# Gated linear attention followed by a dropless mixture of experts: row stores half a pair later, the early gather sooner, first expert units between the last rows

## The chip, the cores and the metric

The kernel runs on one core of a Trainium2 chip. The core has a matrix engine (TensorE, PE in the profile), a vector engine (VectorE, DVE), an activation engine (ScalarE, ACT), a general engine (GpSimd, POOL) and a queue engine that starts most transfers (SyncE, SP). Each engine runs its own instructions in program order and waits where an operand or a buffer is not ready. The metric is the device time of one execution in microseconds, and a smaller number is better. Three executions of the kernel before gave 453.42, 454.57 and 455.56 us.

## The reference

There are two stages. The first is a recurrence with a decaying state for each of 4 x 8 heads, 768 steps and a head size of 48. The second sends each of the 3072 result rows, 384 wide, to one of eight experts.

```python
# first stage, per batch b and head h
for t in range(S):
    state = alpha[t][:, None] * state + outer(k[t], v[t])
    y[t] = q[t] @ state
# x: [4 * 768, 8 * 48], the heads of a token side by side
logits = x @ w_gate                       # [3072, 8]
e = argmax(logits); gate = softmax(logits)[e]
out = gate * (relu(x @ w1[e]) @ w2[e])    # w1[e]: 384 x 1024, w2[e]: 1024 x 384
```

Every token is computed by its expert, however many tokens one expert gets.

## The kernel before

**The attention stage.** The 3072 tokens are cut into NT = 24 chunks of 128, six to a batch element. For each chunk the kernel loads four tiles of 128 x 8 x 48 float32: `a` (alpha), `k`, `q` and `v`. The load of a head row of a token is a piece of 192 bytes. `logs` takes the logarithm of alpha on ScalarE, `cums` sums it over the chunk with a matmul into the one PSUM bank `cum` and makes two exponentials of it (`icp`, `cp`), `operands` multiplies k and q with these on GpSimd, `transposes` turns both with TensorE into the PSUM tile `tp`, from where ScalarE copies kT and VectorE copies qT. `scores` makes kT x qT in the banks `sA` and `sB`; VectorE masks the first into dA, ScalarE copies the second to dB and GpSimd masks it. `products` makes k x v of the chunk, again in `sA` or `sB`, and `state` (GpSimd) folds it into the state `U`. The last row of `cp` goes through DRAM and comes back in another layout: `decay_out` and `decay_in`, both started by ScalarE, so ScalarE waits in `decay_in` until `decay_out` has landed.

**Pairs.** Chunks are worked on two at a time. The loop `for s in range(2, NT - 2, 2)` at L688 emits, for the pair s and s + 1: `reads` (q x state, L408), `weighs` (v x masked scores, L420), `products` of s + 1 and s + 2 (L442), the scores of later chunks, and `rows` (L468), which brings the results back to token order in the one PSUM bank `xr`. `keep_rows` copies a chunk's 128 x 392 rows, with the eight negated logits behind them, to the tile `xs` (ScalarE L475, GpSimd L476); `store_rows` (L481) writes them to the DRAM tensor `x_rows`, and waits for both copies. Everything is emitted by hand in the order in which it is to run on each engine (`manual_schedule`).

**Loads and stores share one queue.** All loads of a, k, q, v, the stores of rows and the weights of the experts are started by SyncE, in the order of the program. `some_loads` names the first ones; after that, `more_loads(n)` takes the next n from the list `to_load`, once at the start of a pair (L689) and once in its middle (L731). Buffers are five deep for a, k and q and six for v.

**Routing.** Chunks form groups of four, with the last four in two groups of two. `choose` finds the expert of each token and `ohs`, the running count per expert (GpSimd, L494). `rank_products` makes the rank of each token within its expert by two matmuls (L499, L500), `slots_of` the slot (VectorE), `one_hots` two 0/1 matrices per chunk, and `tokens_of_slots` multiplies these (L569) so that `slots` (L585) can read off which token stands in which slot. The first two blocks of the first expert are filled from the first sixteen chunks alone: `early_slots` finds them (L531, L537) in pair s = 20, and `fetch_lot(0)` gathers their rows from `x_rows` with two indirect transfers that GpSimd starts (L267).

**The last pair and the experts.** After the loop comes the pair s = 22 (L758 to L826). Between its steps stand the ranks of the last groups, the turning of the two early blocks (L780), and `first_layer` (L796), a generator that emits the first expert layer on the two early blocks, 24 matmuls of 256 columns in eight groups; `go_ahead(n)` takes n steps of it. `fetch_lot(1)` then gathers the other six blocks of that lot, and expert by expert follow `layer1` (L939), `layer2` (L955), `turn_block` (L931) and the scattered stores of the results (L961).

`keep_busy(n)` (L593) is n matmuls of zeros into the `xr` bank, whose results nobody reads.

Of the kernel before, what the change touches and what calls it, by code (L numbers as in the profile page):

```python
# [8 lines left out]
F32 = mybir.dt.float32  # L9
# [9 lines left out]
def kernel(  # L19
# [265 lines left out]
    with tc.tile_pool(name="ld", bufs=6) as ld, \  # L285
# [20 lines left out]
        def some_loads(names):  # L306
            for n in names.split():
                load(n[0], int(n[1:]))


        to_load = [(n, x) for s in range(7, NT + 2) for n, x in (("k", s), ("q", s), ("a", s + 1), ("v", s - 2))]

        def more_loads(n):
            for _ in range(min(n, len(to_load))):
# [2 lines left out]
        def logs(s):  # L317
            st[s]["ln"] = work.tile([C, H, D], F32, name="ln")
            nc.scalar.activation(st[s]["ln"][:], st[s]["a"][:], AF.Ln)
# [38 lines left out]
        def transposes(s):  # L358
            d = st[s]
            for i, n in enumerate(("kT", "qT")):  # L360
                tp = ps.tile([C, NP, C], F32, name="tp", bufs=2)
                for p in range(NP):
                    nc.tensor.transpose(tp[:, p, :], pair(kqb[s % 4][:, i], p), ident[:])  # L363
                d[n] = work.tile([C, NP, C], F32, name=n, bufs=2 + i)
                if i:
                    nc.vector.tensor_copy(d[n][:], tp[:])  # L366
                else:
                    nc.scalar.copy(d[n][:], tp[:])

        def scores(s):  # L370
            d = st[s]
            sA = ps.tile([C, NP, C], F32, name="sA")
            sB = ps.tile([C, NP, C], F32, name="sB")
            for p in range(NP):
                for t, r in ((sA, 0), (sB, DP)):
                    nc.tensor.matmul(  # L376
                        t[:, p, :], lhsT=d["kT"][r : r + D, p, :], rhs=d["qT"][r : r + D, p, :], start=True, stop=True,
                    )
            d["dA"] = work.tile([C, NP, C], F32, name="dA")
            nc.vector.tensor_tensor(d["dA"][:], sA[:], cmask[:, None, :].to_broadcast([C, NP, C]), op=ALU.mult)  # L380
            d["dB"] = work.tile([C, NP, C], F32, name="dB")
            nc.scalar.copy(d["dB"][:], sB[:])
            nc.gpsimd.affine_select(
                d["dB"][:], d["dB"][:], compare_op=ALU.is_ge, fill=0.0,
                base=0, pattern=[[0, NP], [1, C]], channel_multiplier=-1,
            )
# [47 lines left out]
        def products(s):  # L434

            d = st[s]
            if s >= NT or s % NB + 1 == NB:
                return
            kv = ps.tile([C, NP, C], F32, name="s" + "BA"[s % 2])[:, :, :D]
            for p in range(NP):  # L440
                for i, r in enumerate((0, DP)):
                    nc.tensor.matmul(  # L442
                        kv[r : r + DP, p, :], lhsT=kqb[s % 4][:, 0, 2 * p + i, :], rhs=d["v"][:, 2 * p + i, :D],
                        start=True, stop=True,
                    )
            d["acc"] = work.tile([C, NP, D], F32, name="acc" + "BA"[s % 2], bufs=1)
            if s % 2:
                nc.vector.tensor_tensor(d["acc"][:], kv, st[s - 1]["U"][:, :, :D], op=ALU.add)  # L448
            else:
                nc.scalar.copy(d["acc"][:], kv)  # L450
# [20 lines left out]

        def keep_rows(s):
            d = st[s]
            xs = work.tile([C, W], F32, name="xs")
            nc.scalar.copy(xs[:, :Dm].rearrange("t (p c) -> t p c", p=NP), d["xr"][:, :, :D2])  # L475
            nc.gpsimd.tensor_copy(xs[:, Dm:], lgn[:, s, :])  # L476
            d["xs"] = xs
# [146 lines left out]
        operands(1)  # L624
        decay_in(0)
        scores(0)
        some_loads("v1 k2 q2 a3 v2")
        logs(2)
        products(0)
        transposes(1)  # L630
        cums(2)
        decay_out(1)
        operands(2, q=None)
# [1 line left out]
        scores(1)  # L635
        operands(2, None, nc.vector)
        logs(3)
        decay_in(1)
        some_loads("a4 k3 q3 a5 k4")
        decay_out(2)  # L640
        y = results_of(0)
# [10 lines left out]
        transposes(2)  # L652
        cums(3)
        rows(0)
        decay_in(2)
        keep_rows(0)
        operands(3)
        scores(2)
        logs(5)
        state(1)  # L660
        cums(4)
        rows(1)
        decay_out(3)
        some_loads("q4 a6 v3 k5 q5")
        store_rows(0)
        keep_rows(1)
        operands(4)
        transposes(3)
        logs(6)
# [2 lines left out]
        decay_in(3)  # L672
        transposes(4)
        decay_out(4)
        some_loads("v4 k6 q6 a7")
        store_rows(1)
        operands(5)
        cums(6)
        decay_in(4)
# [6 lines left out]
        late_consts(1)  # L686
        parts = fetch_parts(0)
        for s in range(2, NT - 2, 2):  # L688
            more_loads(4 + (s % 6 == 2))  # L689
            y = results_of(s)  # L690
            reads(s)
            reads(s + 1)

            weighs(s, 0)
            weighs(s, 1)
            products(s + 1)
            products(s + 2)
            weighs(s + 1, 0)
            results_to(s, y, 0)
            weighs(s + 1, 1)  # L700
            results_to(s, y, 1)
            state(s + 1)
            state(s + 2)
            do(logs, s + 5)
            scores(s + 2)
            do(logs, s + 6)
            do(cums, s + 5)
            ranks = y[0][:].rearrange("r i p t -> r (i p t)")
            for g in groups_of:
                if g[-1] == s - 1:  # L710
                    slots_of(*rank_products(g, ranks[:, : len(g) * E]))
            counts = ranks[:, C : C + E]
            if s in (TE, ORD):

                nc.tensor.matmul(
                    counts, lhsT=ones_sq[:], rhs=ohs[:, s, :], start=True, stop=True, skip_group_check=True,
                )
            if s == TE + 4:
                early_slots(ranks[:, 2 * C : 2 * C + EB * NQ])
            transposes(s + 3)  # L720
            do(operands, s + 5)
            rows(s)
            keep_rows(s)
            store_rows(s)
            for _ in range(min(2 * (s == ORD), len(hots))):
                one_hots(hots.pop(0))
            do(cums, s + 6)
            do(transposes, s + 4)
            do(decay_out, s + 5)
            do(decay_in, s + 4)  # L730
            more_loads(4 + (s % 6 == 0))  # L731
            rows(s + 1)
            keep_rows(s + 1)
            store_rows(s + 1)
            do(operands, s + 6)
            if s == TE:
                close_early(counts[0:1, 0:1])
            if s == ORD:
                turns(counts[0:1, :])
            scores(s + 3)  # L740
            do(decay_out, s + 6)
            do(decay_in, s + 5)
            late_consts(s)
            late_consts(s + 1)
            for _ in range(min(1 + (s < ORD), len(hots))):
                one_hots(hots.pop(0))
            if s == TE + 4:
                fetch_lot(0)
            for g in groups_of:
                if g[-1] == s + 1:  # L750
                    choose(g)

            for _ in range(6 if s > NT - 6 else 4 if s > NT - 10 else 0):
                next(parts, None)
        for _ in parts:
            pass

        s = NT - 2  # L758
        xT[0] = early.tile([C, DB, CAP], F32, name="xT")
# [2 lines left out]
        y = results_of(s)  # L762
        reads(s)
        reads(s + 1)
        n = len(groups_of[-2]) * E
        r = rank_products(
            groups_of[-2], ps.tile([C, NP, D2 + E], F32, name="xr")[:].rearrange("r p t -> r (p t)")[:, :n],
        )
        weighs(s, 0)
        weighs(s, 1)  # L770
        weighs(s + 1, 0)
        results_to(s, y, 0)
        weighs(s + 1, 1)
        results_to(s, y, 1)
        slots_of(*r)
        one_hots(hots.pop(0))
        for k in range(EB):
            tp = ps.tile([C, NP, C], F32, name="tp", bufs=2)
# [5 lines left out]
        keep_rows(s)  # L784
        store_rows(s)
        tokens_of_slots(NT - 8, NT - 4)
        rows(s + 1)
        keep_rows(s + 1)
        store_rows(s + 1)
        choose(groups_of[-1])  # L790
        while hots:
            one_hots(hots.pop(0))
        banks.close()
        mps = ctx.enter_context(tc.tile_pool(name="moe_ps", bufs=2, space=PSUM))

        def first_layer():  # L796
            for f in range(FB):
                hp = mps.tile([C, CAP], F32, name="hp", bufs=3)
                for a in range(DB):
                    nc.tensor.matmul(  # L800
                        hp[:, :EC], lhsT=w_t[0][0][:, a, f * C : (f + 1) * C], rhs=xT[0][:, a, :EC],
                        start=(a == 0), stop=(a == DB - 1),
                    )
                    yield
                nc.scalar.activation(h_t[0][:, f, :EC], hp[:, :EC], AF.Relu)

        ahead = first_layer()

        def go_ahead(n):
            for _ in range(n):  # L810
                next(ahead, None)

        go_ahead(1)
        slots_of(*rank_products(groups_of[-1], mps.tile([C, Dm], F32, name="zp")[:, : 2 * E]))
        tokens_of_slots(NT - 4, NT - 2)
        go_ahead(6)
# [284 lines left out]
```

## Time and profile before

| what | before |
|---|---|
| median of three executions | 454.57 us |
| span of the profiled execution | 456.1 us |
| TensorE matmuls busy | 428.9 us (94%) |
| GpSimd busy | 142.8 us (31%) |
| VectorE busy | 138.3 us (30%) |
| ScalarE busy | 108.9 us (24%) |
| transfers | 59.41 MB, mean 130 GB/s |

The share of TensorE is that of the whole span. Cut into stages it reads differently: from 183.3 us to the end, the experts, 266.95 of 272.70 us are busy, and from 0 to 183.3 us, the attention stage and the crossing to the experts, 161.98 of 183.30 us. The clock that the throttle granted to TensorE is a column of its own: it is full but for a few stretches of 3.4 or 6.8 us. A wait is printed with the engine that waits and the last thing that it waited for; SPq is the queue of SyncE.

### The profile page before, as it was taken

What the parts mean: (1) busy time and instruction counts of PE and PEld (TensorE: products, weight loads), DVE (VectorE), ACT (ScalarE), POOL (GpSimd) and SP (SyncE); (2) the same over time, 40 slices, a digit from 0 to 9 for tenths busy, and PEclk for the clock granted to TensorE, in tenths of its full rate; (3) what the DMA queues carried; (4) which work ended last, traced back from release to release, by engine and by line L of the source; (5) the groups of instructions that cost most, each with busy time, mean ns of one, the idle gap of its engine ahead of it and who ended that gap; (6) DMA issues with size and microseconds to landing.
All of it is one profiled execution on the core that took longest, in us unless ns stands there. A gap on an engine that the chain in (4) does not pass through costs nothing.

```text
span 456.1 us, 7755 instructions
## 1 busy us (share of the span) xinstructions
PE 428.9 (94%) x2981; PEld 289.6 (63%) x2981; DVE 138.3 (30%) x411; ACT 108.9 (24%) x230; POOL 142.8 (31%) x256
## 2 busy tenths in 40 slices
PE   7989688999999579999999999999999999999994
PEld 5768577888888568855555455665555555555452
DVE  5334344567676643363101110211111101111100
ACT  4455342454553212111011011110110111111011
POOL 2277666557665405015015011005111010010011
PEclk9899998899999979999999999999999999999998
DMA  9994687698985352199554260082270040000000
GB/s 163 180 198 90 141 175 164 127 195 168 206 191 134 99 192 74 36 368 399 184 205 118 86 227 29 1 293 75 67 289 34 1 154 34 1 31 17 2 31 30
DMA packets 128434, 59.41 MB, mean 130 GB/s; under 512 B 110462, under 2 KB 123320, under 8 KB 128394
## 3 DMA queue, kind: packets, MB, share of 16 engines
q1 hardware_dynamic: 116258, 48.87, 41.3%
q0 software_dynamic: 3328, 9.94, 6.6%
q10 hardware_dynamic: 8808, 0.08, 1.1%
q8 instruction: 24, 0.39, 0.4%
q14 instruction: 16, 0.13, 0.1%
HBM read 49.30 MB, written 9.96 MB: 130 GB/s over the span
## 4 chain that ended last, share of the span: by engine, by line
PE 51%; issue 29%; POOL 7%; DMA 7%; DVE 2%; SPq 2%; ACT 1%; POOLq 0%; ACTq 0%
PE zp L955 15%; PE hp L939 13%; PE xr L468 4%; PE sA L376 4%; PE tp L363 4%; PE cum L330 3%; DMA vb<-in_v_dram 3%; PE hp L800 3%; POOL out_dram L961 3%; PE y L420 2%; DMA q_sb<-in_q_dram 1%; SPq L304 1%; DMA xg<-x_rows,g_idx 1%; POOL xg L267 1%; PE xtp L931 1%
## 5 line engine op out<-in xcount | busy, mean ns | idle before, releaser
L955 PE MATMUL zp<-w,h_sb 128*128 128x384 f32 (+2 forms) x560 | 137.1, 487 | 0.0
L939 PE MATMUL hp<-xT,w 128*128 128x416 f32 (+3 forms) x384 | 125.2, 486 | 0.5 <-DVE xT L933 0.5
L955 PEld LDWEIGHTS zp<-w,h_sb 128*128 128x128 f32 (+2 forms) x560 | 73.6, 163 | 56.4 <-issue 14.8
L939 PEld LDWEIGHTS hp<-xT,w 128*128 128x128 f32 x384 | 71.6, 190 | 52.8 <-issue 38.7
L961 POOL DMA_INDIRECT out_dram<-zo,o_idx x26 | 25.8, 994 | 220.7 <-ACT zo L960 195.2
L944 DVE TENSOR_SCALAR h_sb<-hp 128x416 f32<-128x416 f32 (+3 forms) x32 | 17.9, 558 | 149.0 <-PE hp L939 138.5
L960 ACT ACTIVATE zo<-zp,gw 128x384 f32<-128x384 f32 x26 | 15.1, 581 | 123.6 <-PE zp L955 119.1
L946 ACT ACTIVATE h_sb<-hp 128x416 f32<-128x416 f32 (+3 forms) x32 | 15.7, 491 | 106.7 <-PE hp L939 99.3
L376 PE MATMUL sA<-qT,kT 48*128 48x128 f32 x192 | 28.9, 291 | 0.7 <-DVE accA L448 0.5
L376 PE MATMUL sB<-qT,kT 48*128 48x128 f32 x192 | 28.6, 291 | 0.1
L267 POOL DMA_INDIRECT xg<-x_rows,g_idx x26 | 25.2, 971 | 9.8 <-issue 7.2
L420 PE MATMUL y<-dA,vb 128*64 128x128 f32 x192 | 28.1, 292 | 0.0
L354 POOL TENSOR_TENSOR kqb<-k_sb,icp 128x384 f32<-128x384 f32 x23 | 23.0, 1000 | 15.7 <-ACT icp L333 15.7
L376 PEld LDWEIGHTS sA<-qT,kT 48*128 48x128 f32 x192 | 24.0, 193 | 6.0 <-issue 2.7
L363 PE MATMUL tp<-ident,kqb 128*128 128x128 f32 x192 | 27.2, 287 | 0.6 <-POOL kqb L356 0.3
L420 PE MATMUL y<-dB,vb 128*64 128x128 f32 x192 | 27.3, 293 | 0.0
L933 DVE COPY xT<-xtp 128x384 f32<-128x384 f32 (+3 forms) x29 | 13.1, 485 | 46.1 <-PE xtp L931 45.8
L468 PE MATMUL xr<-back,yT 128*128 128x104 f32 x192 | 25.5, 276 | 1.6 <-ACT xs L475 1.6
L363 PEld LDWEIGHTS tp<-ident,kqb 128*128 128x128 f32 x192 | 23.1, 148 | 6.1 <-issue 2.7
L468 PEld LDWEIGHTS xr<-back,yT 128*128 128x128 f32 x192 | 23.7, 193 | 3.0 <-ACT xs L475 2.4
L366 DVE COPY qT<-tp 128x512 f32<-128x512 f32 x24 | 16.6, 691 | 25.8 <-PE tp L363 25.7
L376 PEld LDWEIGHTS sB<-qT,kT 48*128 48x128 f32 x192 | 23.9, 193 | 0.3 <-ACT accB L450 0.3
(172 smaller groups left out, 439.9 us busy)
## 6 DMA issues: line engine op xcount, KB each, us to landing
w<-in_moe_w_dram SPq DMA_DIRECT2D x14, 1536.0 KB
x_rows<-xs SPq DMA_DIRECT2D x24, 196.0 KB
a_sb<-in_alpha_dram SPq DMA_DIRECT2D x24, 192.0 KB
k_sb<-in_k_dram SPq DMA_DIRECT2D x24, 192.0 KB
q_sb<-in_q_dram SPq DMA_DIRECT2D x24, 192.0 KB
vb<-in_v_dram SPq DMA_DIRECT2D x24, 192.0 KB
w<-in_moe_w_dram SPq DMA_DIRECT2D x12, 128.0 KB
w<-in_moe_w_dram SPq DMA_DIRECT2D x8, 192.0 KB
```

Of the source, the lines that this page charges most:

```text
L267: nc.gpsimd.indirect_dma_start(out=xg[:, j, :], out_offset=None, in_=x_d[: N + 1 if n else TE * C + 1, :], in_offset=bass.IndirectOffsetOn ...
L354: k.tensor_tensor(kq[:, 0, :, :D], d["k"][:], heads(d["icp"]), op=ALU.mult)
L363: nc.tensor.transpose(tp[:, p, :], pair(kqb[s % 4][:, i], p), ident[:])
L366: nc.vector.tensor_copy(d[n][:], tp[:])
L376: nc.tensor.matmul(t[:, p, :], lhsT=d["kT"][r : r + D, p, :], rhs=d["qT"][r : r + D, p, :], start=True, stop=True,)
L420: nc.tensor.matmul(d["y"][h][at(p, a) : at(p, a) + DP, n, :], lhsT=d["v"][:, 2 * p + a, :], rhs=d["d" + "AB"[a]][:, p, :], start=(first an ...
L468: nc.tensor.matmul(xr[:, p, :], lhsT=d["yT"][:, p // (NP // 2), p % (NP // 2), :], rhs=back[:, p, :], start=True, stop=True)
L939: nc.tensor.matmul(hp[:, c0:c1], lhsT=w1[:, a, f * C : (f + 1) * C], rhs=xT[:, a, c0:c1], start=(a == 0), stop=(a == DB - 1),)
L944: nc.vector.tensor_relu(h[:, f, c0:c1], hp[:, c0:c1])
L946: nc.scalar.activation(h[:, f, c0:c1], hp[:, c0:c1], AF.Relu)
L955: nc.tensor.matmul(zp[i * wd : (i + 1) * wd, :], lhsT=h[:, f, c : c + wd], rhs=w2[:, f, :], start=(f == 0), stop=(f == FB - 1), skip_group ...
L961: ins = nc.gpsimd.indirect_dma_start(out=out[:, :], out_offset=bass.IndirectOffsetOnAxis(ap=idx, axis=0), in_=zo[:], in_offset=None, bound ...
```

## The change

The edits fall into four kinds. Stores of rows are moved down in the program: `store_rows(s)` and `store_rows(s + 1)` stand half a pair later, `xs` gets a third buffer for that, and the loads are listed with alpha first and taken as 4 + 5 in each pair. In the first pairs, `transposes(1)` goes ahead of `products(0)`, three `keep_busy` matmuls stand ahead of it, and two `decay_in` are moved down. In pair s = 20, `fetch_lot(0)` is emitted directly after `early_slots`, ahead of `slots_of`. In the last pair, `rank_products` moves behind the value products into the bank `sA`, and nine of the 24 steps of `first_layer` are put between and behind the last two `rows`, in the PSUM tiles `tp`; a step now ends with its activation.

```diff
-... for n, x in (("k", s), ("q", s), ("a", s + 1), ("v", s - 2))]
+... for n, x in (("a", s + 1), ("k", s), ("q", s), ("v", s - 2))]
-            xs = work.tile([C, W], F32, name="xs")
+            xs = work.tile([C, W], F32, name="xs", bufs=3)
...
         scores(0)
+        keep_busy(3)
         some_loads("v1 k2 q2 a3 v2")
         logs(2)
+        transposes(1)
         products(0)
-        transposes(1)
...
-        decay_in(1)
         some_loads("a4 k3 q3 a5 k4")
...
         rows(0)
-        decay_in(2)
         keep_rows(0)
+        decay_in(1)
...
         rows(1)
+        keep_rows(1)
         decay_out(3)
+        decay_in(2)
         some_loads("q4 a6 v3 k5 q5")
-        store_rows(0)
-        keep_rows(1)
...
         decay_out(4)
+        store_rows(0)
         some_loads("v4 k6 q6 a7")
-        store_rows(1)
...
         for s in range(2, NT - 2, 2):
-            more_loads(4 + (s % 6 == 2))
+            more_loads(4)
...
-                    slots_of(*rank_products(g, ranks[:, : len(g) * E]))
+            ranked = [rank_products(g, ...) for g in groups_of if g[-1] == s - 1]
...
                 early_slots(ranks[:, 2 * C : 2 * C + EB * NQ])
+                fetch_lot(0)
+            for r in ranked:
+                slots_of(*r)
...
             keep_rows(s)
-            store_rows(s)
+            store_rows(s - 1)
...
-            more_loads(4 + (s % 6 == 0))
+            more_loads(5)
             rows(s + 1)
             keep_rows(s + 1)
-            store_rows(s + 1)
...
             scores(s + 3)
+            store_rows(s)
...
-            if s == TE + 4:
-                fetch_lot(0)
...
         s = NT - 2
         reads(s + 1)
-        r = rank_products(groups_of[-2], ps.tile(..., name="xr")...)
+        store_rows(s - 1)
...
-        slots_of(*r)
+        slots_of(*rank_products(groups_of[-2], ps.tile(..., name="sA")...))
...
         tokens_of_slots(NT - 8, NT - 4)
+        go_ahead(3)
         rows(s + 1)
...
+        go_ahead(6)
         banks.close()
...
-        go_ahead(1)
         slots_of(*rank_products(groups_of[-1], mps.tile([C, Dm], F32, name="zp")[:, : 2 * E]))
```

More of the change, by code (lines that the diff above doesn't have):

```diff
@@ L308, in some_loads @@
                 load(n[0], int(n[1:]))
-        to_load = [(n, x) for s in range(7, NT + 2) for n, x in (("k", s), ("q", s), ("a", s + 1), ("v", s - 2))]
+        to_load = [(n, x) for s in range(7, NT + 2) for n, x in (("a", s + 1), ("k", s), ("q", s), ("v", s - 2))]
         def more_loads(n):
@@ L708 @@
             ranks = y[0][:].rearrange("r i p t -> r (i p t)")
-            for g in groups_of:
-                if g[-1] == s - 1:
-                    slots_of(*rank_products(g, ranks[:, : len(g) * E]))
+            ranked = [rank_products(g, ranks[:, : len(g) * E]) for g in groups_of if g[-1] == s - 1]
             counts = ranks[:, C : C + E]
@@ L756, with first_layer, go_ahead @@
             pass
+        def first_layer():
+            for f in range(FB):
+                if f < 3:
+                    hp = ps.tile([C, NP, C], F32, name="tp", bufs=2)[:].rearrange("r p t -> r (p t)")
+                else:
+                    hp = mps.tile([C, CAP], F32, name="hp", bufs=3)
+                for a in range(DB):
+                    nc.tensor.matmul(
+                        hp[:, :EC], lhsT=w_t[0][0][:, a, f * C : (f + 1) * C], rhs=xT[0][:, a, :EC],
+                        start=(a == 0), stop=(a == DB - 1),
+                    )
+                    if a < DB - 1:
+                        yield
+                nc.scalar.activation(h_t[0][:, f, :EC], hp[:, :EC], AF.Relu)
+                yield
+        ahead = first_layer()
+        def go_ahead(n):
+            for _ in range(n):
+                next(ahead, None)
         s = NT - 2
@@ L764 @@
         reads(s + 1)
[L765 to L768, printed above, removed]
+        store_rows(s - 1)
         weighs(s, 0)
@@ L774 @@
         results_to(s, y, 1)
-        slots_of(*r)
+        slots_of(*rank_products(groups_of[-2], ps.tile([C, NP, C], F32, name="sA")[:, 0, : len(groups_of[-2]) * E]))
         one_hots(hots.pop(0))
@@ L792 @@
             one_hots(hots.pop(0))
+        go_ahead(6)
         banks.close()
         mps = ctx.enter_context(tc.tile_pool(name="moe_ps", bufs=2, space=PSUM))
[L796 to L811, printed above, removed]
-        go_ahead(1)
         slots_of(*rank_products(groups_of[-1], mps.tile([C, Dm], F32, name="zp")[:, : 2 * E]))
```

## The prediction

> **What bounds the kernel now.** I read the busy table by stage first, then what TensorE waited for, then what the SyncE queue waited for, and last the timelines around the largest gaps.
>
> The busy time by stage (stretch, its length, then busy time and count of TensorE, weight loads, VectorE, ScalarE, GpSimd, granted clock, DMA share, GB/s):
>
> ```profile
> 0.00:31.00 31.00, 27.30 (x244) 20.89 (x244) 13.24 (x43) 16.41 (x34) 13.96 (x27) 0.94 1.07 185
> 31.00:88.30 57.30, 48.38 (x636) 41.33 (x632) 25.03 (x63) 23.79 (x53) 35.40 (x84) 0.94 0.66 135
> 88.30:143.20 54.90, 54.16 (x761) 46.98 (x759) 36.53 (x85) 28.19 (x62) 34.93 (x75) 1.00 0.88 180
> 154.60:183.30 28.70, 22.40 (x172) 19.10 (x170) 11.40 (x53) 5.19 (x12) 11.44 (x17) 0.88 0.46 144
> 183.30:456.00 272.70, 266.95 (x1010) 152.51 (x1010) 43.05 (x134) 32.28 (x64) 43.09 (x44) 0.99 0.32 113
> ```
>
> TensorE is the bound everywhere, but it is full only from 88 to 143 us (0.7 us idle in 55) and in the experts. There nothing in this change takes work away, so these 328 us stay. The idle time lies in three places: 3.7 us up to 31, 8.9 us from 31 to 88.3, 6.3 us from 154.6 to 183.3. The clock column gives a second loss: 0.94, 0.94 and 0.88. In finer windows full speed is gone at 12.3-15.7, 77.2-84.0, 159.1-162.5 and 169.4-172.8 us, each at 0.50 and each behind a gap. A stretch of 3.4 us at half speed loses 1.7 us of work: 8.5 us in all. Idle and slow time together are some 29 us, and this is all that a reordering can win.
>
> What TensorE waited for (engine, line, releaser: us in total, times, longest):
>
> ```profile
> PE sB L442 <- DMA vb<-in_v_dram: 6.0, 3, 2.4
> PE xr L499 <- POOL ohs L494: 3.3, 1, 3.3
> PE sB L442 <- ACT dB L382: 2.9, 2, 1.6
> PE xr L468 <- ACT xs L475: 1.6, 2, 0.9
> PE cum L330 <- ACT cp L334: 1.5, 1, 1.5
> ```
>
> The first row is the three late loads of v (48.35, 62.36, 76.28 us). Why they are late stands in the SyncE queue's timeline:
>
> ```profile
> 34.45 0.62 SPq L304 DMA_DIRECT2D k_sb<-in_k_dram  x1
> 42.97 0.34 SPq L481 DMA_DIRECT2D x_rows<-xs  x1
> 43.36 0.45 SPq L304 DMA_DIRECT2D q_sb<-in_q_dram  x1
> 43.85 0.70 SPq L304 DMA_DIRECT2D a_sb<-in_alpha_dram  x1
> 44.65 0.73 SPq L301 DMA_DIRECT2D vb<-in_v_dram  x1
> ```
>
> From 35.1 to 42.97 us the queue stands at a store of rows that are not computed yet, and the loads behind it start 8 us late. Over the whole span `SPq L481 <- ACT xs L475` is 46.1 us in 14 waits. The v of 44.65 is what TensorE waits for at 48.35 (2.40 us); the a of 43.85-48.38 is what ScalarE waits for at 53.81, which gives the 1.46 us at `cum`.
>
> The crossing, on GpSimd and TensorE:
>
> ```profile
> 156.27 1.24 POOL L267 DMA_INDIRECT xg<-x_rows,g_idx  x1 [0.17 <-issue]
> 157.81 0.95 POOL L267 DMA_INDIRECT xg<-x_rows,g_idx  x1 [0.30 <-issue]
> 158.80 0.49 POOL L494 TENSOR_TENSOR ohs<-ohs,oh 128x8 f16<-128x8 f16 x2
> ...
> 159.06 0.17 PE L499 MATMUL xr<-ohs,ones_sq 128*128 128x16 f16 x1 [3.35 <-POOL ohs L494]
> ```
>
> The two gathers stand ahead of `ohs` on GpSimd, the rank matmul waits for `ohs`, and the value products wait behind the rank matmul although their operands were ready at 156.1.
>
> [...]here 1.6 to 3.4 us of idle within a window were enough at four places, while the 2.40 us gap that ends at 48.35 brought none. So I count a lost clock only where it was seen. [...]the 192-byte pieces: the trace moves them at 200 to 230 GB/s at best.
>
> **The change part by part.**
>
> *Stores later, alpha first, 4 + 5 loads.* A pair needs 8 loads of 197 kB and 2 stores of 201 kB, 1.98 MB; at 220 GB/s that is 9 us, and a full pair takes 10.9 us (88.26 to 110.30 us is two). So the transfers fit if the queue doesn't stand. Now the store in mid-pair is that of s - 1, whose copies ended half a pair before, and the one of s comes after five more loads. Taking the program orders side by side, v6, q8 and a9 stand ahead of the store at which they waited, and can start at about 36 us, against 43.4 to 44.7; v then lands 7 us before TensorE wants it. The five-deep buffers allow this: what they replace was consumed a pair ago. It removes 2.40 + 1.39 + 2.21 (v) and 1.46 (alpha), 7.5 us, and with the gap at 76.28 the 6.8 us at half speed that follow it, 3.4 us. Sum 10.9. Against it: in pairs s = 4 and 8 GpSimd has, beside 4.0 us of operands, 1.3 of masks, 1.6 of states, the constants (about 2 us) and the four `ohs` (1.04), some 10 us of a pair of 11. It becomes the next bound there, and I take off 0.5. Range 6 to 11.5; value 10.4.
>
> *First pairs.* Before, TensorE is idle for 1.62 us up to 11.92 and then at half speed to 15.7. The three dummies take three times 0.45 us (32 records of L800, sixteen matmuls of the same 256 columns, took 7.15 us at full speed) and lie in the gap. k and q of chunk 1 are ready at 10.5 and 11.5, so the transposes run at 11.6-12.5, the products of chunk 0 (copy of dB ended 11.87) to 12.95, `cum` to 13.6, and the scores of chunk 1 start at about 13.7 against 15.81. The later `decay_in` takes a wait of 2.66 us off ScalarE, whose work wasn't due. The chain behind (GpSimd, 23.45 to 31.75 without a pause) starts at the rows of chunk 0 and moves with it. Loads are near their limit here (DMA share 1.07), but q5 and k6 start some 5 us before use. Value 2.0, range 0.5 to 2.5.
>
> *Gather sooner, ranks behind the counts.* In pair 20 TensorE loses 0.73 us in front of the count and 0.93 in front of the second `rows`. VectorE is busy without a pause from 148.3 to 151.7 and its work stays the same, so the two merge and nothing is won; one 0.29 at 127.6 goes. The gathers move from 156.3-158.8 to about 149.7-152: no `xs` copy (due 151.8) waits long behind them. They land before 155 instead of at 164. Value 0.3.
>
> *Last pair.* Value products at once: 155.7-157.5. `ohs` follows the choice (VectorE ends it at 157.33) at 157.85, so the rank matmul waits 0.4. Then 6 transposes (0.7), 16 token products (0.9), `rows` 22 (0.9), 4 token products (0.4): 161.0. Three steps of the first layer, 3 x 0.44, cover the copy of `xs` (before: 0.70 idle): 162.3; `rows` 23 to 163.2, against 168.4. Six steps, 2.6 us, cover the choice of the last group (1.3 us) and `ohs` (0.5). About 0.5 goes in handing over the PSUM banks, since the rank's tile waits for the activation. Rank at 166.4, six more steps, last token products 169.5, `slots(0)` 169.8-170.5, first gather issued at 170.8. Before, the one issued at 175.62 had its last packet at 178.5, so this one lands at 173.7 and the second 1.25 us later. Only 24 - 15 = 9 steps are left to cover it: 169.65-173.5. So TensorE waits about 0.2 and 0.9 for the two blocks and 0.6 for their copies, and `layer1` starts at 175.9 instead of 183.26: 7.35 us, and both half-speed windows are in it. A new one behind the new waits would cost 1.7; at one in four I take 0.4. Value 6.9, range 3.5 to 8.
>
> The remaining edits (third `xs` buffer, activation emitted with its step) cost nothing: ScalarE is idle for over 60% of these stages.
>
> Sum: 10.4 + 2.0 + 0.3 + 6.9 = 19.6 us, and 454.57 - 19.6 = 435.0.
>
> **Rivals.**
> 1. *GpSimd and ScalarE become the bound in pairs 2 to 8.* For it: GpSimd's 10 us a pair above, and ScalarE's wait in `decay_in` behind the 1.27 us gap of TensorE at 34.92, which stays. Against it: from 88 us the same chains keep TensorE full at 10.9 us a pair, and GpSimd is busy only 35.4 of 57.3 us between 31 and 88. Two or three gaps of 1 to 1.5 us come back with one slow window: the front gives 5 instead of 12.4, 454.57 - 12.2 = 442.4.
> 2. *The crossing pays its filler back.* The nine steps that were moved up are missing under the gather of the next lot. If it lands 2.4 us later than computed and a slow window follows (1.7), the last pair gives 7.35 - 4.1 = 3.3: 438.6.
> 3. *No gain or slower.* Early loads crowd out the small decay transfers, ScalarE stands longer in `decay_in`, and every pair waits for its state: 0.9 us more in each of ten pairs, less the crossing's 6.9, gives 456.7. For it: DMA share 1.07 in the first 31 us. Against it: the share is 0.66 from 31 to 88, and 0.88 in the stretch where TensorE is full.
>
> **How the numbers follow.** The forecast 0.63, rival 1 0.16, rival 2 0.14, rival 3 0.07. The low end is all parts at their best, 11.5 + 2.5 + 0.5 + 8 = 22.5, and 1 us of spread: 431.0. The high end takes in rivals 1 and 2: 443.5. Faster by over 0.5%, 0.93; within, 0.03; slower, 0.04, the last two from rival 3.
>
> **What would show it.** Right: no wait of `sB` products for v of over 0.5 us; the queue's waits of L481 for `xs` far below 46.1 us; clock 1.00 in 31-78 us; the gathers of lot 0 ahead of the `xs` copies of pair 20; nothing in front of the last value products; `layer1` of the first expert near 164 us on the new clock (183.3 - 19.6); from there to the end 272 to 273 us as before. Wrong: gaps behind `U`, `dB` or `kqb` from GpSimd in the first pairs (rival 1); over 2 us in front of L931 or L939 of the first expert (rival 2); longer waits for `Eb` (rival 3).

## The result and the profile after

| what | before | after |
|---|---|---|
| median of four executions | 454.0 us | 440.48 us |
| ratio after / before | | 0.971 (95%: 0.966 to 0.977) |
| span of the profiled execution | 456.1 us | 437.9 us |
| mean granted clock in it | 0.977 | 0.995 |
| TensorE matmuls busy in it | 428.9 us (94%) | 423.9 us (97%) |

The changed kernel is 13.5 us faster by the medians; the forecast was 19.6. The profiled execution of the kernel before took 457.88 us and is not one of the four; that of the changed kernel, 439.68 us, is the fastest of its four. The two are 18.2 us apart, and the difference between 13.5 and 18.2 is the first thing to explain below. Ratios here and below leave out an execution over 1.5% slower than the fastest of its kernel (one of e2, 453.87 us, and two of the kernel before, 460.06 and 459.5 us).

The busy time by stage of the changed kernel, with the stretches cut at the same points of the work (reads of pair 2, of pair 10, of pair 20, of the last pair, first `layer1`); columns as before, pair 20 itself (131.8 to 142.4) left out:

```profile
0.00:32.20 32.20, 27.96 (x250) 21.60 (x250) 13.23 (x43) 16.20 (x34) 13.95 (x27) 1.00 1.08 186
32.20:77.90 45.70, 45.11 (x630) 38.98 (x628) 26.84 (x63) 23.62 (x53) 35.07 (x84) 1.00 0.93 184
77.90:131.80 53.90, 53.59 (x765) 46.78 (x763) 36.27 (x85) 28.04 (x62) 34.91 (x75) 1.00 0.83 170
142.40:163.50 21.10, 19.07 (x171) 16.18 (x170) 11.14 (x53) 5.47 (x13) 7.80 (x14) 1.00 0.55 171
163.50:437.90 274.40, 268.68 (x1010) 154.33 (x1010) 43.07 (x134) 31.85 (x63) 44.41 (x46) 0.99 0.32 113
```

Pairs 2 to 8, 57.2 us before, take 45.7, with TensorE full and the clock at 1.00. The crossing from the last reads to `layer1` takes 21.1 us in place of 28.7. The first stretch is no shorter: pair 2 starts at 32.2 instead of 31.1 us. From pair 10 to the last reads (77.9 to 142.4) it is 64.5 us against 66.3. In the experts some 1.6 us were lost.

What TensorE waits for now (engine, line, releaser: us in total, times, longest):

```profile
PE tp L363 <- POOL kqb L354: 2.5, 1, 2.5
PE xr L598 <- DVE still L115: 1.2, 1, 1.2
PE xr L468 <- ACT xs L475: 1.1, 1, 1.1
PE xtp L933 <- DMA xg<-x_rows,g_idx: 1.0, 2, 0.7
PE hp L941 <- DVE xT L935: 0.5, 1, 0.5
```

The waits for v, for `cp` and for `ohs` are gone. New are 2.5 us for the operands of chunk 4 and 1.0 us for the gathered rows.

The SyncE queue, to be read against the 8 us stop of before:

```profile
35.67 0.77 SPq L301 DMA_DIRECT2D vb<-in_v_dram  x1
36.90 0.70 SPq L304 DMA_DIRECT2D a_sb<-in_alpha_dram  x1
43.14 0.34 SPq L481 DMA_DIRECT2D x_rows<-xs  x1
43.53 0.34 SPq L195 DMA_DIRECT2D x_rows<-zero_w  x1
43.91 0.39 SPq L304 DMA_DIRECT2D k_sb<-in_k_dram  x1
```

The queue still stands for 5.5 us at a store (`L481 <- ACT xs` is 30.9 us over the span, against 46.1), so the forecast's "far below 46.1" was not a good sign to look for. What has changed is what stands behind the store: v was issued at 35.67, ahead of it, and the load that waits now is one for the next pair. The 5.5 us of standing cost nothing here, since what the queue held back wasn't due: TensorE has no gap of over 0.4 us from 31 to 139 us.

### The profile page after: what moved, and what is told of

It is laid out like the page before. It is cut to its first block, busy times and chain, and to the rows that moved or that the text cites. A ratio compares the mean times of both kernels' runs of the same rounds, so it can differ in the third digit from the quotient of the medians.

```text
span 437.9 us, 7756 instructions
## 1 busy us (share of the span) xinstructions
PE 423.9 (97%) x2987; PEld 286.5 (65%) x2987; DVE 139.3 (32%) x411; ACT 108.2 (25%) x230; POOL 142.3 (32%) x256
## 4 chain that ended last, share of the span: by engine, by line
PE 55%; issue 30%; POOL 5%; DMA 4%; DVE 2%; SPq 2%; ACT 1%; ACTq 1%; POOLq 0%; DVEq 0%
PE zp L957 15%; PE hp L941 14%; PE sA L376 4%; PE xr L468 4%; PE y L420 4%; PE tp L363 3%; PE cum L330 3%; POOL out_dram L963 3%; PE y L408 2%; POOL xg L267 1%; SPq L304 1%; PE xtp L933 1%; DMA k_sb<-in_k_dram 1%; PE tp L763 1%; DMA q_sb<-in_q_dram 1%
## 5 line engine op out<-in xcount | busy, mean ns | idle before, releaser
L941 PE MATMUL hp<-xT,w 128*128 128x416 f32 (+3 forms) x384 | 126.9, 492 | 0.5 <-DVE xT L935 0.5
L941 PEld LDWEIGHTS hp<-xT,w 128*128 128x128 f32 x384 | 73.3, 194 | 52.6 <-issue 38.6
L948 ACT ACTIVATE h_sb<-hp 128x416 f32<-128x416 f32 (+3 forms) x32 | 15.7, 490 | 111.9 <-PE hp L941 111.9
L376 PE MATMUL sA<-qT,kT 48*128 48x128 f32 x192 | 28.1, 286 | 0.5 <-DVE accA L448 0.3
L363 PE MATMUL tp<-ident,kqb 128*128 128x128 f32 x192 | 25.5, 275 | 2.8 <-POOL kqb L354 2.5
L376 PE MATMUL sB<-qT,kT 48*128 48x128 f32 x192 | 27.7, 285 | 0.3 <-ACT accB L450 0.3
L363 PEld LDWEIGHTS tp<-ident,kqb 128*128 128x128 f32 x192 | 21.8, 141 | 8.1 <-POOL kqb L354 3.1
L935 DVE COPY xT<-xtp 128x384 f32<-128x384 f32 (+3 forms) x29 | 13.1, 484 | 44.1 <-PE xtp L933 44.0
L376 PEld LDWEIGHTS sA<-qT,kT 48*128 48x128 f32 x192 | 23.3, 187 | 5.2 <-issue 1.7
L420 PE MATMUL y<-dA,vb 128*64 128x128 f32 x192 | 25.8, 277 | 0.0
L420 PE MATMUL y<-dB,vb 128*64 128x128 f32 x192 | 25.2, 277 | 0.0
L376 PEld LDWEIGHTS sB<-qT,kT 48*128 48x128 f32 x192 | 23.1, 187 | 0.5 <-ACT accB L450 0.5
```

Of the source, the lines that this page charges most:

```text
L376: nc.tensor.matmul(t[:, p, :], lhsT=d["kT"][r : r + D, p, :], rhs=d["qT"][r : r + D, p, :], start=True, stop=True,)
L420: nc.tensor.matmul(d["y"][h][at(p, a) : at(p, a) + DP, n, :], lhsT=d["v"][:, 2 * p + a, :], rhs=d["d" + "AB"[a]][:, p, :], start=(first an ...
L941: nc.tensor.matmul(hp[:, c0:c1], lhsT=w1[:, a, f * C : (f + 1) * C], rhs=xT[:, a, c0:c1], start=(a == 0), stop=(a == DB - 1),)
L948: nc.scalar.activation(h[:, f, c0:c1], hp[:, c0:c1], AF.Relu)
```

## The experiments

Each kernel ran beside the kernel before, and a ratio is against that kernel's median on the same chip (455.2, 456.74 and 454.82 us in the three groups). The crossing is the time from the last reads to the first `layer1` in the profile.

| label | median us | ratio (95%) | crossing us |
|---|---|---|---|
| the change | 440.48 | 0.971 (0.966-0.977) | 21.1 |
| e1_stores | 449.57 | 0.987 (0.981-0.993) | 30.7 |
| e2_crossing | 447.75 | 0.984 (0.977-0.990) | 21.3 |
| e3_after_decay_back | 438.96 | 0.964 (0.959-0.969) | 21.2 |
| e4_after_first_pairs_before | 439.71 | 0.965 (0.959-0.970) | 21.3 |
| e5_gather_late | 449.26 | 0.985 (0.979-0.992) | 29.8 |
| e6_ranks_first | 444.5 | 0.977 (0.970-0.984) | 23.2 |
| e7_no_steps_ahead | 443.19 | 0.971 (0.964-0.977) | 21.7 |
| e8_shorter_chain | 436.02 | 0.958 (0.952-0.963) | 19.9 |
| e9_old_load_list | 439.01 | 0.965 (0.959-0.971) | 21.3 |
| e10_two_xs | 442.2 | 0.974 (0.966-0.982) | 21.2 |
| e11_e8_no_dummies | 434.87 | 0.957 (0.951-0.964) | 19.9 |

**e1, the stores alone.** The kernel before with the late stores, the third buffer and the new load list; first pairs, but for their stores, and crossing as before.

```diff
             keep_rows(s)
-            store_rows(s)
+            store_rows(s - 1)
...
             scores(s + 3)
+            store_rows(s)
```

> The kernel before with the later stores, alpha first, 4 + 5 loads and the third xs buffer alone. Theory (stores in front of loads made v and alpha late): the waits of sB products for v (6.0 us) and of cum for cp (1.5 us) go, the first layer1 still starts some 28 us behind the last reads; 6 to 9 us less than before, 445 to 448. Rival (the gaps were only the visible part; the time came from slow clock windows that come and go between executions): under 3 us less, 451 to 454, with the v waits gone all the same.

Measured: 5.6 us less. No wait for v or for `cp` is left, and pair 10 starts at 78.4 us in place of 88.3. The crossing took 30.7 us, and behind its gap of 3.34 us TensorE runs at half speed from 149.8 to about 158.6 us (one value product, L420, takes 0.42 us there and 0.27 at full speed), where the profiled execution of before had one stretch of 3.4 us; 2.0 us of what the front won were lost there in this execution. The size is just short of the expected 6 to 9 us; the place of the gain is as expected.

**e2, the crossing alone.**

```diff
                 early_slots(ranks[:, 2 * C : 2 * C + EB * NQ])
+                fetch_lot(0)
...
-        r = rank_products(groups_of[-2], ps.tile(..., name="xr")...)
         weighs(s, 0)
...
+        slots_of(*rank_products(groups_of[-2], ps.tile(..., name="sA")...))
```

(and the first-layer steps, as in the change.)

> The kernel before with the crossing alone: gather of lot 0 directly behind early_slots, ranks behind the value products, nine first-layer steps between the last rows. Theory: from the last reads to layer1 of the first expert 20 to 21 us in place of 28.7, everything up to there as before; 5.5 to 8 us less, 446 to 448.5, and e1 and e2 add up to what the whole change gave (13.5). Rival (the filler that was moved up is paid back under the next gather): under 4 us less.

Measured: 7.45 us less, crossing 21.3 us, v waits still there (4.3 us). With e1 the sum is 13.05 us, against 13.5 for the whole change. The parts add up within their spread (each interval reaches some 3 us to either side), and nothing that can be seen is left over for the edits of the first pairs.

**e3 and e4, the first pairs.** e3 puts two `decay_in` of the changed kernel back (the diff shows that of chunk 1; that of chunk 2 goes back ahead of `keep_rows(0)`); e4 puts back all of the first pairs but the stores.

```diff
         logs(3)
+        decay_in(1)
         some_loads("a4 k3 q3 a5 k4")
...
         keep_rows(0)
-        decay_in(1)
```

> The changed kernel with both decay_in of the first pairs at their old places. Theory (GpSimd's state of chunk 1 waits for a decay row that was asked for 4 us later, and the operands of chunk 4 stand behind it): the 2.17 us of GpSimd and the 2.47 us of TensorE in front of the transposes of chunk 4 go, reads of pair 2 start near 29.8 us in place of 32.2; 1.5 to 2.5 us less than the changed kernel, 438 to 439. Rival (ScalarE's wait in decay_in comes back and delays the same chain): the same time as the changed kernel within 0.7 us.

> The changed kernel with the first pairs as before (no dummies, transposes of chunk 1 behind the products, both decay_in early), its later stores kept. Theory: the edits of the first pairs came out near nothing, +1.0 at the scores of chunk 1 and -2.2 by the late decay_in, so within 1 us of the changed kernel, 439.5 to 441.5. Rival (the forecast's 2 us were there and something later ate them): 2 us more, 442.5.

Measured: 438.96 and 439.71 us, ratios 0.964 and 0.965 against 0.971; the intervals overlap, so no more is shown than that the first pairs' edits together bring no gain that can be seen. Their working is seen in the traces. GpSimd in the changed kernel:

```profile
24.50 0.63 POOL L383 TENSOR_SCALAR_AFFINE_SELECT dB<-dB 128x512 f32<-128x512 f32 x1
27.30 0.51 POOL L459 TENSOR_TENSOR Ub<-accA,Eb 128x192 f32<-128x192 f32 x1 [2.17 <-DMA Eb<-decay_rows]
27.74 0.19 POOL L476 COPY xs<-lgn 128x8 f32<-128x8 f32 x1
27.89 1.00 POOL L354 TENSOR_TENSOR kqb<-k_sb,icp 128x384 f32<-128x384 f32 x1
```

and in e4, with the decay rows asked for at their old place:

```profile
25.41 0.64 POOL L383 TENSOR_SCALAR_AFFINE_SELECT dB<-dB 128x512 f32<-128x512 f32 x1
26.02 0.51 POOL L459 TENSOR_TENSOR Ub<-accA,Eb 128x192 f32<-128x192 f32 x1
26.47 0.19 POOL L476 COPY xs<-lgn 128x8 f32<-128x8 f32 x1
26.61 1.01 POOL L354 TENSOR_TENSOR kqb<-k_sb,icp 128x384 f32<-128x384 f32 x1
```

The state of chunk 1 is not itself in a hurry, but the operands of chunk 4 stand behind it on the same engine, and TensorE's transposes behind those. In e3 the 2.17 and 2.47 us are gone and pair 2 starts at 30.7 instead of 32.2 us, but by pair 4 only 0.4 us of it are left (43.6 against 44.0): there a gap of 1.36 us stands in front of the products (0.29 in the changed kernel), because ScalarE's copy of dB comes behind `decay_in(4)`, which waits for its row: sent at 30.82 us, it is fetched at 33.17, and the copy starts at 34.04. So both sides of the expectation had a part: the wait went, and the next one in the same chain took most of its place. It need not: e4 also has the decay rows early, has no such gap in its profile and starts pair 4 at 42.6 us. What makes the difference between e3 and e4 there was not tested.

**e5, e6, e7: the crossing edit by edit.** Each takes one edit of the crossing back.

```diff
e5:              early_slots(ranks[...])
e5: -            fetch_lot(0)
...
e6: +    r = rank_products(groups_of[-2], ps.tile(..., name="sA")...)
e6:      weighs(s, 0)
...
e7:      tokens_of_slots(NT - 8, NT - 4)
e7: -    go_ahead(3)
e7:      rows(s + 1)
...
e7: -    go_ahead(6)
e7:      banks.close()
...
e7: +    go_ahead(1)
```

> The changed kernel with the gather of lot 0 at its old place, after the last scores of pair 20. Theory (the gather is what makes the crossing short: ohs stands behind it on GpSimd, and its rows land some 7 us after the issue while the weights of the first expert are on their way): the transposes of the early blocks wait 3 to 4 us, rank products 1.6; from the last reads to layer1 26 to 28 us in place of 21.1, 444 to 448 us. Rival (the order of the rank products alone did it): within 2 us of the changed kernel, 439 to 442.5.

Measured: 449.26 us, 8.8 above the change (6.4 by the ratios, 0.985 against 0.971 of 454.0, since the two ran on different chips), and a crossing of 29.8 us, longer than in the kernel before. TensorE in e5:

```profile
148.57 0.17 PE L499 MATMUL sA<-ohs,ones_sq 128*128 128x16 f16 x1 [1.44 <-issue]
151.84 0.90 PE L799 MATMUL tp<-ident,xg 128*128 128x128 f32 x3 [3.07 <-DMA xg<-x_rows,g_idx]
154.04 0.90 PE L799 MATMUL tp<-ident,xg 128*128 128x128 f32 x3 [1.30 <-DMA xg<-x_rows,g_idx]
```

3.07 + 1.30 us for the gathered rows, and TensorE at half speed from the end of the first of these gaps to about 157.5 us (the eight matmuls of `rows` at 156.44 take 1.61 us, the next eight, at 159.47, 1.03). It is slower than the 444 to 448 us expected. The gather's early start is what the crossing's gain rests on; value products at once, without it, only reach the wait for its rows sooner.

> The changed kernel with the rank products of the last pair ahead of its value products again, the early gather kept. Theory: TensorE stands from the end of the reads until ohs, some 2.1 us, and all behind it moves by that: from the last reads to layer1 23 us in place of 21.1, 441.5 to 444 with a slow window now and then. Rival (ohs is early enough now that its gather is gone from in front of it): within 0.7 us of the changed kernel.

Measured: 444.5 us (ratio 0.977 against 0.971, 2.7 us, with intervals that overlap) and a crossing of 23.2 us, 2.1 more than the change, with the one gap that was expected:

```profile
147.77 0.17 PE L499 MATMUL sA<-ohs,ones_sq 128*128 128x16 f16 x1 [1.96 <-POOL ohs L494]
```

> The changed kernel with no first-layer steps between the last rows; they follow the old way, one ahead of the last ranks, six behind, the rest under the gather. Theory (the steps only move the idle time: what they fill in front of the last ranks they leave open under the gather): waits of 0.7 and 0.9 us in front of the last rows and the first step come back, the 0.3 + 0.7 us for the gathered rows go, and layer1 starts within 1 us of the changed kernel's 21.1 behind the last reads; 439.5 to 442. Rival (the forecast's account, in which the steps gain 0.7 + 0.9 and a slow window): 3 us more, 443.5.

Measured: a crossing of 21.7 us and the same ratio as the change, 0.971. TensorE in e7:

```profile
155.43 1.14 PE L468 MATMUL xr<-back,yT 128*128 128x104 f32 x8 [0.61 <-ACT xs L475]
157.49 0.70 PE L760 MATMUL hp<-xT,w 128*128 128x256 f32 x2 [0.93 <-ACT xs L475]
158.79 0.22 PE L569 MATMUL cum<-oh_c,oh_r 128*128 128x128 f16 x1 [0.23 <-DVE oh_c L562]
170.48 1.70 PE L937 MATMUL hp<-xT,w 128*128 128x192 f32 x9 [0.61 <-ACT h_sb L766]
```

2.4 us of gaps, and none for gathered rows; the changed kernel has 0.48 in front of the last ranks, 0.32 + 0.66 for the rows and 0.54 for their copies, 2.0 us. The nine steps moved the idle time from in front of the ranks to under the gather and won 0.6 us of crossing in these two profiles. The median of e7 is 2.7 us above that of the change, which is the rival's figure, but e7 was timed beside 456.74 us for the kernel before and the change beside 454.0; by the ratios nothing is left of it.

**e9, e10: what in the stores' part is needed.**

```diff
e9:  -  ... (("a", s + 1), ("k", s), ("q", s), ("v", s - 2))]
e9:  +  ... (("k", s), ("q", s), ("a", s + 1), ("v", s - 2))]
e10: -            xs = work.tile([C, W], F32, name="xs", bufs=3)
e10: +            xs = work.tile([C, W], F32, name="xs")
```

(e9 also has the old counts of loads.)

> The changed kernel with the load list and the counts of before (k, q, alpha, v; 4 + 4 and a fifth now and then), its later stores kept. Theory (the place of the stores is what made v and alpha late, not the order among the loads): no wait for v over 0.5 us, within 1 us of the changed kernel, 439.5 to 441.5. Rival (alpha first is what took the 1.5 us at cum and its slow windows away): 2 to 3 us slower, 442.5 to 443.5.

> The changed kernel with two xs buffers instead of three. Theory (a store half a pair later holds its buffer half a pair longer, so the copy of s + 1 has to wait until the store of s - 1 has landed[...], and the xr bank with it): waits of TensorE in front of the second rows of pairs, 0.5 to 1.5 us in each of ten, 446 to 455 us, most of the gain of the later stores gone. Rival (the store has landed by then, the third buffer is only caution): within 1 us of the changed kernel.

Measured: e9 439.01 us with no wait for v or `cp`: the stores' place did it, the order of the loads nothing that can be seen. e10 442.2 us, ratio 0.974: the expected waits in front of the second rows are not there (32.6 to 145.8 us hold 3.9 us of idle TensorE, and none of it for a store), so my theory was wrong, and that the third buffer is needed can't be seen at this precision.

**e8 and e11: a faster version.** The crossing is a chain: last rows, choice, count, rank, slots, gather. e8 leaves thirteen steps under the gather instead of nine, shortens the chain ahead of it, and takes VectorE's slot work of pair 20 out from in front of its first rows. Its decay rows come early, but `decay_in(4)` behind the scores that it delayed in e3. The diff shows neither the early decay rows nor the move of `slots_of`.

```diff
-        decay_in(4)
         scores(3)
+        decay_in(4)
...
         tokens_of_slots(NT - 8, NT - 4)
+        while hots:
+            one_hots(hots.pop(0))
         go_ahead(3)
         rows(s + 1)
...
-        go_ahead(6)
+        go_ahead(3)
+        tokens_of_slots(NT - 4, NT - 2)
         banks.close()
...
-        go_ahead(6)
-        one_hots(hots.pop(0), nc.gpsimd)
+        go_ahead(5)
+        one_hots(hots.pop(0))
```

> A version meant to be faster. Against the changed kernel: decay_in of chunks 1 and 2 early and that of chunk 4 behind the scores of chunk 3; slots_of of pair 20 behind its first rows; one-hot rows of chunks 20 and 21 and their token products ahead of the last choice; six instead of nine first-layer steps ahead of the last ranks, five instead of six behind, so that thirteen are left under the gather; both last one-hots on VectorE. Theory (the crossing is a chain from the last rows through choice, count, rank, slots and gather, and steps of the first layer must fill it without lengthening it): the waits for the gathered rows go, the 1.1 us in pair 20 go, layer1 19 us behind the last reads, 436 to 438.5. Rival (TensorE is full otherwise, and gaps only move): 439.5 to 441.

> The faster version e8 without the three dummy matmuls ahead of the transposes of chunk 1. Theory (they hold the clock): a gap of 0.8 to 1.3 us at 10.5 us and in most executions a slow window behind it, 0.5 to 1.5 us more than e8, 436.5 to 438. Rival (with the transposes ahead of the products the gap is short enough, and the clock is held without them): as e8 or up to 0.5 us less.

Measured: e8 436.02 us, ratio 0.958, whose interval (0.952 to 0.963) lies below that of the change. It overlaps that of e3 (0.959 to 0.969), so how much of the gain belongs to the shorter chain and how much to the early decay rows isn't shown. What TensorE waits for in it:

```profile
PE xr L468 <- ACT xs L475: 2.0, 2, 1.2
PE xr L598 <- DVE still L115: 1.3, 1, 1.3
PE sB L376 <- ACT accB L450: 1.1, 3, 0.5
PE hp L945 <- DVE xT L939: 0.9, 1, 0.9
```

There is no wait for gathered rows, and the crossing takes 19.9 us, not the 19 expected. The wait in pair 20 went from 1.10 to 0.79 only. e11, without the dummies, has a gap of 0.43 + 0.30 us where they were, pair 2 at 29.2 against 30.7 us, and 434.87 us; e8 and e11 cannot be told apart (0.958, 0.957). The dummies aren't needed once the transposes go first: my theory there fell.

## Why the prediction was right, and where its terms were off

The measured 440.48 us lies in the range, the direction is right, and the mechanism of both large parts is as argued. The total was 6.1 us too good.

In the traces the sum came out almost to the letter: `layer1` starts 19.7 us earlier (163.53 against 183.26), and 19.6 was forecast. That it is so close is luck. The first pairs gave 1.15 us less than nothing in place of 2.0; pairs 2 to 8 gave 11.5 for 10.4, pairs 10 to 20 1.8 for 0.3, the crossing 7.5 for 6.9, and the errors cancel. Of the 19.7 us the experts lost some 1.6; the rest of the way to 13.5 is 3.9 us by which the profiled execution of before lay above its median and 0.8 us by which that of the changed kernel lay below its own. Step by step:

*The starting point* (454.57 - 19.6). The savings were read from an execution that took 457.88 us and were subtracted from a median of 454.57. How much that matters shows over 23 other executions of the kernel before, whose time falls with the mean granted clock: a line through them goes from 457.4 us at 0.977 to 453.5 at 0.989, 0.33 us for each 0.001. The profiled execution had 0.977, the middle one of those had 0.982. So some of the half-speed windows that I counted in (12.3, 77.2, 159.1, 169.4 us, 8.5 us of work) were probably not in the typical execution, and could not be won there: 3.3 us at 454.57, 3.9 at 454.0. From 457.88 the same 19.6 us give 438.3, and the profiled execution of the changed kernel took 439.68. This is the largest single term of the miss that nothing made up for. It is worked out from clock and time, not from traces of the other executions, which show only these two numbers.

*Stores later (10.4).* Right in mechanism: pairs 2 to 8 went from 57.2 to 45.7 us, 11.5, with the waits for v and `cp` at zero, and e9 confirms that it was the stores' place. By medians e1 gives 5.6. In e1's own profile pairs 2 to 8 take 47.3 us, 9.9 less than before; 2.0 of this were lost in its crossing and 0.4 in pairs 10 to 20, and 2.7 are the distance of the profiled execution of before from the median that e1 is compared with, less 0.9 by which e1's profile lay above e1's median. About 1 us of the 11.5 does not come from the stores: the gap of 1.27 us at 34.92, of which rival 1 said that it stays, is still 1.29 in e1, but 0.29 in the changed kernel. GpSimd did not become the bound (rival 1): no gap behind `U` or `kqb` from pair 2 on.

*First pairs (2.0).* Wrong: pair 2 starts 1.15 us later, not 2 us earlier, and e4, without these edits, is no slower. Counted from the first reads to those of pair 2, so that a later start of the kernel doesn't matter, the four kernels with the old first pairs (before, e1, e2, e4) take 13.1 us and the changed one 15.2. The step that failed is "the later `decay_in` takes a wait of 2.66 us off ScalarE, whose work wasn't due", and with it "the chain behind ... moves with it". I asked who stood behind the old wait on ScalarE and not who waits for the row: GpSimd's state of chunk 1, with the operands of chunk 4 behind it. The other edits did in part what was said: the scores of chunk 1 started at 14.80 in place of 15.81 (13.7 was forecast), and 12.3-15.7 us are at full clock. ScalarE won nothing. This is the wait of 2.66 us, before and in the changed kernel:

```profile
20.72 0.32 ACT L450 COPY accB<-sB 128x192 f32<-128x192 f32 x1 [2.66 <-DMA Eb<-decay_rows]
19.70 0.32 ACT L450 COPY accB<-sB 128x192 f32<-128x192 f32 x1 [2.66 <-PE sB L442]
```

It is as long as it was, now put down to the products. The copy reads these products, and in both traces it starts 0.10 us behind their end (20.62 and 19.60 us). So `decay_in` never was what ScalarE waited for last, though the profile named it, and moving it could free nothing there.

*Gather sooner in pair 20 (0.3).* The 0.73 and the 0.93 us merged, as said, though into 1.10 and not into their sum of 1.66. That it is worth no more than 0.3 was wrong by attribution: its worth is in the last pair, where e5 loses 6 to 9 us without it.

*Last pair (6.9).* Right: `layer1` starts 21.1 us behind the last reads; the working said 21.3, from 154.6 to 175.9 on the old clock. Waits of 0.32 + 0.66 + 0.54 us were forecast as 0.2 + 0.9 + 0.6, the bank hand-over of 0.5 came as 0.48. The half-speed window that I gave one chance in four came in this execution, at 164 us:

```profile
160.00:163.80 3.80, 2.28 (x13) 1.38 (x12) 1.48 (x5) 0.42 (x2) 2.89 (x4) 1.00 0.59 163
163.80:167.40 3.60, 3.60 (x15) 3.60 (x14) 0.40 (x2) 0.33 (x1) 1.10 (x2) 0.57 0.48 143
167.40:171.00 3.60, 3.60 (x23) 3.60 (x23) 0.72 (x2) 0.33 (x1) 0.00 (x0) 0.96 0.01 4
```

(as the table by stage). 15 matmul records run in 3.6 us where 23 follow in the next: this is about the 1.6 us that the experts lost. It stands behind 1.52 us of short gaps, and e3, with 0.32 + 0.78 + 0.54 us, has none; of the six kernels with this crossing (the change, e2, e3, e4, e9, e10) three have one in their profile (in e4 and e9 the first 48 matmuls of `layer1` take 9.72 us, in e3 and e10 8.04). Rival 2 (filler paid back) was right about the mechanism, as e7 shows, but the payback was already in the sum.

*The rest.* From pair 10 to the last reads I forecast 0.3 and the two profiled executions differ by 1.8; the other kernels of this study take 64.8 to 67.8 us there with the same work, so this is spread, not gain. Two smaller readings of the prediction were off without harm: ScalarE is idle for 47, 58 and 49% of the first three stretches of its table, not for over 60%, and a full pair takes 11.0 us, not 10.9.

## What to carry to other kernels

In a queue that holds loads and stores in program order, what counts is what stands behind a store that isn't ready; move the store down until the loads due next are ahead of it, and don't count the time that the queue stands (here v was issued at 35.67 us in place of 44.65, and 30.9 us of standing were left). Before moving a small transfer later because its issuing engine waits in it, ask who waits for its data, and what else stands behind that wait (2.17 us on GpSimd became 2.47 us on TensorE); and look when the other operands of the waiting instruction were ready, because the wait may be theirs. Steps that fill a latency chain help only where they don't leave its next wait empty (with the nine steps moved up 2.0 us of gaps, without them 2.4); and when savings are read from one trace, subtract them from that execution's own time, not from a median with another clock.

## What the runs showed of the hardware that was not expected

The half-speed stretches of TensorE are not a fixed cost of a gap. In the traces of before and of the changed kernel they are 3.41 or 6.83 us long at a clock of 0.50, those at the very end left out, and within each of the two the changes of the clock lie whole multiples of 3.41 us apart (before: 12.25, 15.67, 77.11, 83.93, 159.03, 162.44, 169.27 and 172.68 us). But practically the same gap gives anything from no half-speed stretch to one of 10.2 us. Behind the gap of 2.4 to 2.5 us in front of the transposes of chunk 4, the changed kernel and e5 have none (its clock is full up to 164.3 us in the one, and the scores behind the gap, L376, take 0.27 us each in the other); e6, e9 and e10, with gaps of 2.3 to 2.6 us there, have some 3.4 us (the scores take 0.42 us each in e6 and e9, the two matmuls of `cum` 1.62 us in e10, against 0.86 in e5); and e7, with 2.4, has 10.2 us:

```profile
28.00:29.50 1.50, 0.99 (x7) 0.75 (x8) 0.00 (x0) 1.30 (x4) 1.50 (x3) 0.99 0.96 173
29.50:39.70 10.20, 10.20 (x109) 8.18 (x109) 1.74 (x3) 2.83 (x8) 6.20 (x13) 0.50 1.22 202
39.70:47.00 7.30, 7.30 (x74) 6.28 (x72) 3.75 (x7) 4.65 (x11) 4.45 (x9) 1.00 0.26 63
```

From 29.5 to 39.7 us TensorE is busy all the time at 0.50. The kernels with the decay rows early (e3, e4, e8, e11) have no gap over 0.3 us there, and no half-speed stretch behind it either (scores of 0.27 us each).

What differs is where a gap lies, as far as these two traces show it. Divide each into windows of 3.41 us, counted from a change of its clock; the first border then lies at 2.01 us before and at 0.46 us in the changed kernel, so the same work lies differently in the windows. In the changed kernel the gap (26.47 to 28.94 us) is then split at 27.77 us, and the two windows that share it hold 1.30 and 1.47 us of idle TensorE. These are the windows at full clock with over 1.2 us of idle TensorE, those at both ends of the kernels left out:

| kernel | followed by half speed, idle us | not followed by it, idle us |
|---|---|---|
| before | 1.85, 2.21, 3.32, 1.48 | 1.96, 1.46, 1.39, 1.27 |
| changed | 1.52 | 1.47, 1.30 |

Several short gaps within one window were followed by it too: the 1.52 us of the changed kernel, between 160.9 and 164.3, are 0.32 + 0.66 + 0.54. Idle time in the window is not all of it, as the 1.96 us (before, 46.4 to 49.8) show. The same gap in front of chunk 4's transposes then cost its own length alone or, at half of each stretch, an estimated 1.7 (e6, e9, e10) to 5 us (e7) more. How the windows lay in the other executions isn't shown, and why e7 stays at half speed for 10.2 us is open.
